# A mixer kernel of two layers: low parts stored a step later, and z updates moved out of the third block product

## The chip, the cores and the metric

The kernel runs on one core of one Trainium2 chip. The metric is the device time of one launch in microseconds, the median of several runs; lower is better. The engines are called as in the profile: PE (matrix products; PEld is its weight load), DVE (vector), ACT (scalar), POOL (GpSimd) and SP (which only issues DMAs here). Each engine works through its own queue in order; a DMA is issued from the queue of SP, POOL or ACT and lands later.

## The reference

```python
def _A_ref(x, wqkv, wo):                       # linear attention, 32 heads of 16
    qkv = (x @ wqkv).reshape(B, S, 3, H, Dh).transpose(2, 0, 3, 1, 4)
    phi = lambda t: jnp.where(t > 0, t + 1, jnp.exp(t)) + 1e-6
    pq, pk = phi(q), phi(k)
    kv = einsum("bhsd,bhse->bhde", pk, v);  z = pk.sum over s
    o = einsum("bhqd,bhde->bhqe", pq, kv) / (einsum("bhqd,bhd->bhq", pq, z) + 1e-6)
    return o.reshape(B, S, D) @ wo

def _B_ref(x, w_in, w_sp, b_sp, w_out):        # gated MLP, mixing over tokens
    z = gelu(x @ w_in)                         # 2048 x 1792
    z1, z2 = z[..., :896], layernorm(z[..., 896:])
    g = einsum("ts,bsf->btf", w_sp, z2) + b_sp # 2048 x 2048 times 2048 x 896
    return (z1 * g) @ w_out

for _ in range(2):                             # two layers, same weights
    x = x + _A_ref(layernorm(x), wqkv, wo)
    x = x + _B_ref(layernorm(x), w_in, w_sp, b_sp, w_out)
```

x is 2048 x 512 in fp32, all weights are fp32.

## The kernel before, in words

Every product is made of three PE matmuls on rounded operands: an operand is split into a high part (ACT, `high`, L223: a copy to fp32r) and a low part (DVE, `low`, L226: the operand minus its high part), and `mm3` (L237 to L239) adds high x high, high x low and low x high in a PSUM bank. Splits that are used more than once can be kept in DRAM and loaded again; those are the arrays `lows` (lowP in the profile).

The order of all instructions is written out by hand: the program is one long list, and each engine takes its share of it in that order. Buffers come from small pools handed out first in, first out: 22 pages (128x512), 6 quads (128x2048), 4 bigs, 8 PSUM banks. The 16 blocks of 128 tokens are called tiles; loops run over steps s, in which different tiles stand at different stages.

Each layer has three phases.

1. Class `P1`, the projection phase: a step per tile with layernorm (`ln_a`, `ln_b`), a turn of the tile through DRAM and DVE's block transposition (`Turn`: the store at L429, the load at L205, `pre` with the transposition at L458), the split of the turned tile (`T_high`, `T_low`), then the products K, Q and Gmm (36 matmuls of 128x512 in a step). In layer two (`self.L` is 1) the loop also makes the low parts of w_sp blocks that the third phase wants: `keepload` (L1671) fetches a quad of w_sp, `keep` makes its high and low part in the next step and stores the low part (L1681), six pieces in all. `wk` and `wq` hold four of the six quads in this loop.
2. Class `P2`, the token steps: attention output, second layernorm, gelu of both halves. `e`/`e2` make z (tiles `ztile[0..15]`, 128x896 each), `e3` its statistics (a square on ACT, L1101, and three small POOL instructions), `e4` normalises it. Layer one runs `run`; layer two runs `run2`, which takes tiles in pairs (`epair` in even steps, `odd` in odd steps; `epair` holds L1036 and L1042, DVE's sums between two groups of PE). Near the end, `first_a`, `first_b`, `T1`, `tail` make the last quarter of the gelu half by a scheme of seven products (Strassen and Winograd). In layer one `FSums` loads pieces of w_in (L205), splits them a step later (L745 to L748) and stores the sums two steps later (L761).
3. Class `P4`, the token mixing w_sp x z2, by seven block products in the order P2, P1, P6, P7, P4, P5, P3. In layer two P2, P1, P4 and P5 are divided again into seven, 14 steps of 12 matmuls each (`mm_div`, `evac_div`); the others have 8 steps of 18 matmuls (`mm`, `evac`). Each step needs a w_sp operand, split or loaded (`wsp`: ACT L1811, DVE L1814, or for kept pieces POOL's DMA L1817), and a z operand (`zsp` for undivided products: ACT L1877, DVE L1879 or L1881). The scheme updates z in place as it goes: in P6 of layer two `zsp` first replaces the second half of z tile k (H2, 384 columns) by H1 - H2 (L1855) and adds H2 of tile k + 8 (L1856), and then splits it. `run` works ahead: `sp(g + 2)` prepares operands two steps on, `zahead` those of the divided products. `tick` multiplies gates in between (POOL L2090 or DVE L2088).

```python
                if not evac_first and not div_first:
                    self.sp(g + 2)
                    self.zahead(g + (3 if p == "P5" or not early and g < 6 else 4))
                self.mm(g)
```

With `div_first` the evacuation of a divided product's last step stands ahead of `sp(g + 2)`; before, that holds in P4 alone.

Of the kernel before, what the change touches and what calls it, by code (L numbers as in the profile page):

```python
# [96 lines left out]
KEPT = ("P7", "P5", "P1")  # L97
KEEP = 1


# [61 lines left out]
def mixer_kernel(ctx: ExitStack, tc: tile.TileContext, x_in, wqkv, wo_d, win1_d, win2_d, wsp_d, bsp_d, wout_d,  # L162
# [300 lines left out]
    class P1:  # L463
# [187 lines left out]
        def run(self, sums):  # L651
            side = deque([self.win2] * NF)
            ND = NT - DEFER
            for s in range(1, NT + 2):
# [46 lines left out]
                if s == 14:  # L701
                    self.wo = quads.get([P, 4, 512])
                    nc.sync.dma_start(self.wo, wo_d.rearrange("(c p) f -> p c f", p=P))
                if s in range(3,NT-1):
                    self.turn.pre(s + 1)
# [3 lines left out]
                if self.L:  # L709
                    sums.keep()  # L710
                    if s >= KEEP:
                        sums.keepload()
                    if s <= NT:
                        sums.halve(40 + (s - 1) // 2, None, (s - 1) % 2)
                    if 9 <= s < NT + 1:
                        sums.halve(28 + (s - 9) // 2, None, (s - 9) % 2)
                    if s <= 4:
                        self.win2.load(2)
                    else:
                        self.win2.piece()  # L720
                    if s == NT - 1:
                        self.win2.sums()
                    if s == NT:
                        self.win2.last()
                    continue
# [113 lines left out]
    class P2:  # L839
# [498 lines left out]
        def run(self, sums):  # L1338
# [4 lines left out]
            for s in range(1, NT + 3):  # L1343
                if s in (15, 16, 17):
                    self.first_a(s - 15)
                self.loadx(s + 1)
                if s < 5:
# [56 lines left out]
                if s >= 3:  # L1404
                    if s < NT:
                        self.e(s - 3)
                        self.e2(s - 3)
                    if s != NT + 1:
                        self.e3(s - 3)
                for _ in range(FONE.get(s, 0)):  # L1410
                    self.f()
                if s in (15, 16, 17):
                    self.first_b(s - 15)
                    self.first_out(s - 15)
                if s - 2 in WADD:
                    self.fsums.store()
                if s in WADD:
                    if not WADD[s]:
                        self.fsums = FSums()
                    self.fsums.load(WADD[s])  # L1420
                if s - 1 in WADD:
                    self.fsums.split(WADD[s - 1])
# [26 lines left out]
        def odd(self, s, p, q, r):  # L1449
# [34 lines left out]
            if s == NT + 1:  # L1484
                self.first_b(1, 2)
                self.T1()

        def run2(self):
# [129 lines left out]
    class Sums:  # L1618
# [3 lines left out]
        def __init__(self):  # L1622
# [9 lines left out]
            for p in DIVIDED[1]:  # L1632
                for q in range(2):
                    for m in range(1, 5):
                        self.halves[p, m, q] = dram.tile([2, P, 512], F32, name=f"h{p}_{m}_{q}")
            self.parts = [(what, p, m, q) for p in ("P4", "P5", "P1") for what in ("copy", "add") for m in (1, 3, 2, 4)
                          for q in range(2)]
            self.unkept, self.split = deque((j, s + 2 * q) for j, s in ((0, 0), (0, 4), (1, 4)) for q in range(2)), None

# [34 lines left out]
        def keep(self):  # L1674

            if self.split is not None:
# [3 lines left out]
                low(r.bitcast(F32R), r, h)  # L1680
                nc.sync.dma_start(at, r)  # L1681
                quads.put(t)
# [60 lines left out]
    class P4:  # L1743
# [81 lines left out]
        def kept(self, g):  # L1825
            p, k = self.steps[g]
            if p not in KEPT or p == "P7" and k < 4 or p == "P1" and not self.L:
                return None
# [10 lines left out]
        def zsp(self, g):  # L1839
# [13 lines left out]
            elif p == "P6":  # L1853
                if "P1" in self.div:
                    nc.vector.tensor_sub(a[:, H2], a[:, H1], a[:, H2])  # L1855
                    nc.vector.tensor_add(a[:, H2], a[:, H2], b[:, H2])  # L1856
                z, sign = a[:, H2], -1.0
# [25 lines left out]
            if tmp is not None:  # L1883
                pages.put(tmp)
            self.z[g] = (h, l)

        def zdiv(self, p, half, side, q, i):
# [497 lines left out]
        def run(self, nxt):  # L2385
# [17 lines left out]
            for g in range(n):  # L2403
                p, k = self.steps[g]
                self.fetch(g + 5)
                evac_first = p == "P6" and k == HT - 1
                div_first = p in self.div and k == 13 and p == "P4"
                if not evac_first and not div_first:
# [12 lines left out]
                if p in self.div:  # L2421
# [7 lines left out]
                    if k == 13 and p == "P4":  # L2429
                        self.gq.extend((n, f) for n in range(2) for f in range(3))  # L2430
                    if p == "P1":
                        if k == 10:
                            self.ask(3)
# [110 lines left out]
```

## Time and profile before

| what | value |
|---|---|
| time, median of 3 runs | 1352.46 us (1351.88 to 1354.0) |
| profiled execution: time, span | 1353.23 us, 1351.4 us |
| granted PE clock | 1.00 of full speed |
| busy share of the span: PE, PEld, DVE, ACT, POOL | 99%, 84%, 79%, 56%, 36% |
| HBM read and written | 224.26 MB, 114.03 MB (250 GB/s) |
| DMA queue of SP and ACT (q1), of POOL (q0): share of 16 DMA engines | 59.6%, 16.1% |
| largest DMA groups of 512 KB | qd<-s x62, qd<-hP x48, qd<-in_wsp_dram x44 |

The profile names an instruction by its line in the listing above (L226), its engine, its operation and its tiles, out<-in: pg are pages, qd quads, bg bigs, z_z a z tile, bank a PSUM bank. A row of a timeline has the start in us from the span's start, the length in us, and in brackets the idle time of the engine before it with the instruction that ended it. A row of waits has the waiting instruction, the one it waited for, the us in total, the number of waits and the longest. Matmuls overlap: each is drawn 0.39 us long though the next starts earlier.

### The profile page before, as it was taken

Reading aid. Unit: us, or ns where it says so; the run is one execution under the profiler, and the core shown is the slowest. Engines: PE = TensorE matmul, PEld = TensorE weight load, DVE = VectorE, ACT = ScalarE, POOL = GpSimd, SP = SyncE. Lnnn points to the kernel's source line nnn. Section 1 sums busy time; section 2 is a strip of 40 time slices with the busy share of each in tenths; the row PEclk is TensorE's granted clock in tenths of the full one; section 3 lists DMA queues with packets and bytes.
Section 4 is the critical chain, followed back from the end, with each engine's and each line's share of the span. In section 5 each row is a group of like instructions: output and inputs, shape, how many; then the busy total and the mean of one; then the engine's idle time right before and its main releaser. Section 6 shows DMA issues by size and latency. Waiting matters only on the chain.

```text
span 1351.4 us, 19331 instructions
## 1 busy us (share of the span) xinstructions
PE 1333.4 (99%) x6493; PEld 1131.2 (84%) x6493; DVE 1073.5 (79%) x1729; ACT 757.0 (56%) x1278; POOL 480.1 (36%) x633
## 2 busy tenths in 40 slices
PE   9999999999999999999998999999999999999999
PEld 7888888888888888889986788888888876888898
DVE  6779866558899689888857778677689879899885
ACT  5764534446742364445666765556688633666454
POOL 3754765533035400302433554554431022112021
PEclk9999999999999999999999999999999999999999
DMA  5898588887889987895988883678768865679354
GB/s 183 287 316 277 189 264 297 285 265 245 256 268 372 316 273 224 286 330 148 203 201 240 205 203 96 215 251 249 242 202 250 258 225 184 176 237 318 129 77 66
DMA packets 183348, 314.43 MB, mean 233 GB/s; under 512 B 15440, under 2 KB 56400, under 8 KB 182864
## 3 DMA queue, kind: packets, MB, share of 16 engines
q1 hardware_dynamic: 161216, 266.65, 59.6%
q0 software_dynamic: 21888, 46.41, 16.1%
q8 instruction: 51, 0.84, 0.3%
q14 instruction: 49, 0.40, 0.1%
q10 hardware_dynamic: 144, 0.13, 0.0%
HBM read 224.26 MB, written 114.03 MB: 250 GB/s over the span
## 4 chain that ended last, share of the span: by engine, by line
PE 84%; DVE 6%; DMA 5%; ACT 2%; issue 1%; SPq 1%; POOL 1%; ACTq 0%; POOLq 0%; DVEq 0%
PE bank L2051 11%; PE bank L2049 11%; PE bank L2050 11%; PE bank L239 10%; PE bank L237 10%; PE bank L238 10%; PE bank L2250 3%; PE bank L2251 3%; PE bank L2252 3%; DMA pg<-xt 2%; DMA yt<-z_y 1%; PE bank L1169 1%; PE bank L1171 1%; PE bank L1170 1%; PE bank L998 1%
## 5 line engine op out<-in xcount | busy, mean ns | idle before, releaser
L2049 PE MATMUL bank<-qd,pg 128*128 128x512 f32 x704 | 274.8, 390 | 4.1 <-ACT pg L1877 1.7
L2051 PE MATMUL bank<-qd,pg 128*128 128x512 f32 x704 | 274.6, 390 | 0.2 <-DVE pg L1879 0.2
L2050 PE MATMUL bank<-qd,pg 128*128 128x512 f32 x704 | 274.0, 389 | 0.0
L1811 ACT ACTIVATE qd<-qd 128x1024 fp32r<-128x1024 f32 x148 | 155.5, 1052 | 87.6 <-PE bank L2051 41.1
L1814 DVE TENSOR_TENSOR qd<-qd,qd 128x1024 fp32r<-128x1024 f32 x132 | 169.5, 1286 | 29.5 <-ACT qd L1811 29.3
L239 PE MATMUL bank<-qd,pg 128*128 128x512 f32 x448 | 174.7, 390 | 0.0
L2049 PEld LDWEIGHTS bank<-qd,pg 128*128 128x128 f32 x704 | 132.1, 188 | 34.0 <-ACT pg L1877 3.7
L2051 PEld LDWEIGHTS bank<-qd,pg 128*128 128x128 f32 x704 | 132.1, 188 | 29.5 <-DVE pg L1881 1.3
L2050 PEld LDWEIGHTS bank<-qd,pg 128*128 128x128 f32 x704 | 132.1, 188 | 27.3
L237 PE MATMUL bank<-qd,pg 128*128 128x512 f32 x264 | 103.5, 392 | 6.5 <-DVE pg L226 6.3
L238 PE MATMUL bank<-qd,pg 128*128 128x512 f32 x264 | 103.0, 390 | 0.0
L239 PEld LDWEIGHTS bank<-qd,pg 128*128 128x128 f32 x448 | 84.1, 188 | 18.0 <-DVE pg L226 0.4
L1712 POOL TENSOR_TENSOR pg<-pg,pg 128x512 f32<-128x512 f32 x48 | 69.7, 1453 | 71.6 <-DVE pg L1879 51.5
L2090 POOL TENSOR_TENSOR bg<-bg,pg 128x512 f32<-128x512 f32 x28 | 49.4, 1767 | 127.0 <-ACT qd L1811 120.7
L372 POOL TENSOR_SCALAR rs<-mv 128x1 f32<-128x1 f32 x76 | 23.6, 311 | 177.3 <-DVE mv L370 173.4
L223 ACT ACTIVATE pg<-pg 128x512 fp32r<-128x512 f32 (+1 forms) x94 | 55.2, 595 | 51.3 <-DVE pg L1908 21.0
L2252 PE MATMUL bank<-wo,qd 128*128 128x256 f32 x288 | 81.4, 283 | 0.0
L2250 PE MATMUL bank<-wo,qd 128*128 128x256 f32 x276 | 78.1, 283 | 0.0
L2251 PE MATMUL bank<-wo,qd 128*128 128x256 f32 x276 | 78.0, 283 | 0.0
L458 DVE STREAM_TRANSPOSE bank<-pg 128x512 f32<-128x512 f32 x58 | 41.5, 716 | 35.6 <-DMA pg<-yt 21.7
L237 PEld LDWEIGHTS bank<-qd,pg 128*128 128x128 f32 x264 | 49.6, 188 | 18.5 <-DVE pg L226 8.1
L226 DVE TENSOR_TENSOR pg<-pg,pg 128x512 fp32r<-128x512 f32 (+1 forms) x92 | 59.7, 658 | 6.2 <-ACT pg L223 5.7
(308 smaller groups left out, 3420.9 us busy)
## 6 DMA issues: line engine op xcount, KB each, us to landing
qd<-s SPq DMA_DIRECT2D x62, 512.0 KB, 4.4
qd<-hP SPq DMA_DIRECT2D x48, 512.0 KB, 4.7
qd<-in_wsp_dram SPq DMA_DIRECT2D x44, 512.0 KB, 4.4
pg<-z SPq DMA_DIRECT2D x56, 256.0 KB, 5.1
pg<-in_wsp_dram SPq DMA_DIRECT2D x52, 256.0 KB, 4.7
s<-pg SPq DMA_DIRECT2D x48, 256.0 KB, 4.4
z<-pg SPq DMA_DIRECT2D x40, 256.0 KB, 3.6
pg<-w POOLq DMA_DIRECT2D x38, 256.0 KB, 5.2
```

The costliest lines, as they stand in the source:

```text
L237: nc.tensor.matmul(out, ah, bh, start=start, stop=False)
L238: nc.tensor.matmul(out, ah, bl, start=False, stop=False)
L239: nc.tensor.matmul(out, al, bh, start=False, stop=stop)
L1712: nc.gpsimd.tensor_tensor(t, a, b, op=OP.add)
L1811: self.mark = nc.scalar.activation(w[:, 0], r, AF.Copy)
L1814: nc.vector.tensor_sub(w[:, 1], r, w[:, 0].bitcast(F32))
L2049: m(out, h[:, o], w[:, 0, j, :], start=start, stop=False, skip_group_check=True)
L2050: m(out, h[:, o], w[:, 1, j, :], start=False, stop=False, skip_group_check=True)
L2051: m(out, l[:, o], w[:, 0, j, :], start=False, stop=stop, skip_group_check=True)
L2250: m(out, A, x, start=start and f == 0, stop=False, skip_group_check=True)
L2251: m(out, A, y, start=False, stop=False, skip_group_check=True)
L2252: m(out, B, x, start=False, stop=stop and f == 2, skip_group_check=True)
```

## The change

Three edits, two of them in layer two alone.

- The projection phase of layer two: `keep` moves ahead of the turn (`turn.pre`) in the step and no longer stores; a new `keepstore`, at that place in the next step, stores the low part and gives the quad back. Five pieces are made instead of six, and `kept` no longer names step 13 of product P1, whose low part is made on DVE when it is used.
- Product P6 of layer two: its two updates of z leave `zsp`. The eight subtractions become `hsub`, two in each of the odd token steps 9, 11, 13 and 15; the eight sums become `hadd`, two in token step 17 and six in steps 1, 2, 4, 5, 7 and 8 of product P1. `div_first` now holds for step 13 of P1 as well.
- The token steps of layer one: the statistics `e3` of tiles 11, 12 and 13 move from the middle of steps 14, 15 and 16 to the start of steps 15, 16 and 17, behind `first_a`; and in steps 13 to 17 the load of w_in pieces stands ahead of the store of the sums.

```diff
+HADD = {1: 2, 2: 3, 4: 4, 5: 5, 7: 6, 8: 7}
...
+                if self.L:
+                    sums.keepstore()
+                    sums.keep()
                 if s in range(3,NT-1):
                     self.turn.pre(s + 1)
...
                 if self.L:
-                    sums.keep()
                     if s >= KEEP:
                         sums.keepload()
...
                 if s in (15, 16, 17):
                     self.first_a(s - 15)
+                    self.e3(s - 4)
...
-                    if s != NT + 1:
+                    if s < 14 or s > NT + 1:
                         self.e3(s - 3)
...
-                if s - 2 in WADD:
-                    self.fsums.store()
                 if s in WADD:
                     if not WADD[s]:
                         self.fsums = FSums()
                     self.fsums.load(WADD[s])
+                if s - 2 in WADD:
+                    self.fsums.store()
...
             if s == NT + 1:
                 self.first_b(1, 2)
                 self.T1()
+                self.p4.hadd(0, 1)
+            elif s >= 9:
+                self.p4.hsub(s - 9, s - 8)
...
-            self.unkept, self.split = deque((j, s + 2 * q) for j, s in ((0, 0), (0, 4), (1, 4)) for q in range(2)), None
+            self.unkept = deque(((0, 0), (0, 2), (0, 4), (0, 6), (1, 4)))
+            self.split, self.due = None, None
...
                 low(r.bitcast(F32R), r, h)
-                nc.sync.dma_start(at, r)
+                self.due = t, at
+
+        def keepstore(self):
+            if self.due is not None:
+                (t, at), self.due = self.due, None
+                nc.sync.dma_start(at, t[:, 0])
                 quads.put(t)
...
-            if p not in KEPT or p == "P7" and k < 4 or p == "P1" and not self.L:
+            if p not in KEPT or p == "P7" and k < 4 or p == "P1" and (not self.L or k == 13):
                 return None
...
             elif p == "P6":
-                if "P1" in self.div:
-                    nc.vector.tensor_sub(a[:, H2], a[:, H1], a[:, H2])
-                    nc.vector.tensor_add(a[:, H2], a[:, H2], b[:, H2])
                 z, sign = a[:, H2], -1.0
...
+        def hsub(self, *ks):
+            for k in ks:
+                a = ztile[k]
+                nc.vector.tensor_sub(a[:, self.H2], a[:, self.H1], a[:, self.H2])
+
+        def hadd(self, *ks):
+            for k in ks:
+                a, b = ztile[k], ztile[k + HT]
+                nc.vector.tensor_add(a[:, self.H2], a[:, self.H2], b[:, self.H2])
...
-                div_first = p in self.div and k == 13 and p == "P4"
+                div_first = p in self.div and k == 13 and p in ("P1", "P4")
...
                     if p == "P1":
+                        if k in HADD:
+                            self.hadd(HADD[k])
```

## The prediction

> **What bounds the kernel now.** I read the page first: busy time by engine, then the chain that ended last, then TensorE's (PE's) waits, then stretches of the timeline around each wait.
>
> ```profile
> span 1351.4 us, 19331 instructions
> PE 1333.4 (99%) x6493; PEld 1131.2 (84%) x6493; DVE 1073.5 (79%) x1729; ACT 757.0 (56%) x1278; POOL 480.1 (36%) x633
> PE 84%; DVE 6%; DMA 5%; ACT 2%; issue 1%; SPq 1%; POOL 1%; ACTq 0%; POOLq 0%; DVEq 0%
> ```
>
> PE is busy for 1333.4 of 1351.4 us, so no edit can win more than some 18 us unless it takes matmuls away, and this one takes none. The chain says where the rest lies: 16% of it runs outside PE, in places where PE just catches up with somebody. What is to be won are PE's waits, all of which the next view names (us in total, times, longest):
>
> ```profile
> PE bank L237 <- DVE pg L226: 6.3, 4, 1.8
> PE bank L2049 <- ACT pg L1877: 1.7, 4, 0.5
> PE bank L2049 <- DVE bg L2109: 1.6, 1, 1.6
> PE bank L239 <- DVE qd L226: 1.0, 1, 1.0
> PE bank L2049 <- DVE bg L1996: 0.8, 1, 0.8
> PE bank L1952 <- DMA qd<-lowP: 0.5, 1, 0.5
> PE bank L2051 <- DVE pg L1879: 0.2, 1, 0.2
> ```
>
> These rows fall into three places. The four waits on the low part of K's operand (L226) are the early steps of layer two's projection phase (class P1). The ones on L1877, L2109, L1996, lowP and L1879 (eight waits, 4.8 us) stand in the block products P1, P6 and P7 of layer two. L239 on L226 (1.0 us) is the last token step but one of layer one's class P2. A wait costs more than its idle time, as PE's own timeline shows:
>
> ```profile
> 707.80 0.39 PE L239 MATMUL bank<-qd,pg 128*128 128x512 f32 x1
> 711.20 0.39 PE L239 MATMUL bank<-pg,pg 128*128 128x512 f32 x1
> 712.91 0.50 PE L237 MATMUL bank<-qd,pg 128*128 128x512 f32 x1 [1.32 <-DVE pg L226]
> 713.25 0.40 PE L238 MATMUL bank<-qd,pg 128*128 128x512 f32 x1
> ```
>
> Fifteen matmuls started from 707.80 to 711.20, one each 0.227 us. The next came 1.71 us later, a loss of 1.48 for 1.32 idle, since the page draws a matmul 0.39 long; and the one after it took 0.34 instead of 0.227. So I add 0.27 us to each wait: 0.16 for overlap and 0.11 for the restart.
>
> **Part A: low parts in the projection phase (keep, keepstore).** In layer two's class P1 each step loads a quad of w_sp, makes its low part (ACT L223, DVE L226) and stores it from SP (L1681). The chain that ended last goes round in it:
>
> ```profile
> 714.47 5.25 DMA pg<-xt
> ...
> 720.37 1.21 DVE qd L226
> ...
> 722.02 0.47 SPq L1671
> ...
> 722.53 0.87 SPq L311
> ...
> 724.04 4.75 DMA pg<-xt
> ```
>
> ```profile
> SPq L1681 <- DVE qd L226: 28.5, 6, 6.8
> DMA to landing us min/median/max: 3.2/3.5/4.5
> ```
>
> The turned block lands, DVE turns it (L458), the low part stands behind that on DVE, the store waits for it at the head of SP's queue (28.5 us for six stores), and the load of the next turned block stands behind the store. One round takes 9.6 us (714.47 to 724.04), while a step is 36 matmuls, 8.2 us on PE. This is the whole of the four waits. The change breaks it in two places. The low part is made ahead of the turn, so it no longer waits for the block, and T's low part is no longer 1.2 us behind it. The store goes out a step later, when its low part is long done, so SP does not wait for DVE there.
>
> What is late next: the quads. Four of six hold wk and wq, two go round. Before, a quad was stored a step ahead of its next load; now store and load of one buffer follow each other on SP, and the load (L1671) has to wait until the store has landed, 3.5 us by the row above (the second line there is of the stores L1681). That holds in steps 3, 4 and 5. Behind it stand the two w_in loads, x's load and the load of the turned block. The new round goes over two steps. Landing of the block 5.0, from its turn to the store of the block two on 5.4 (L458 at 709.63, L429 at 715.00), then on SP 0.37 for that store, as much for the keep's, the landing L, 0.47 for L1671, and 1.5 from there to the block's next load (722.53 to 724.04):
>
> ```profile
> 709.63 0.73 DVE L458 STREAM_TRANSPOSE bank<-pg 128x512 f32<-128x512 f32 x1 [3.45 <-DMA pg<-xt]
> 715.00 0.37 SPq L429 DMA_DIRECT2D xt<-pg  x1
> ```
>
> That is 13.1 + L; with L at 3.5 a round of 16.6 for two steps, 8.3 each, 0.1 over PE's 8.2, over three held steps some 0.4 us, and with L at 4.5 1.9 us. The sixth piece falls away, with a load and a store of 512 KB, a high part and a low part of 1.2 us; its cover was DVE's step at 747, where the fourth wait stood. The four waits cost 6.3 + 4 x 0.27 = 7.4; I leave 1.5 in place, nearer to the upper case, since the store now runs among the same step's loads, and take **-5.9** (ends: -7.4, and -4.4 if L goes a little over 4.5).
>
> **Part B: z updates and P1's last evacuation, layer two.** In P6 the subtraction and the sum stood in front of each step's high part:
>
> ```profile
> 1108.59 1.23 DVE L1814 TENSOR_TENSOR qd<-qd,qd 128x1024 fp32r<-128x1024 f32 x1 [0.39 <-ACT qd L1811]
> 1109.73 1.65 DVE L1855 TENSOR_TENSOR z_z<-z_z 128x384 f32<-128x384 f32 x1
> 1111.41 0.56 DVE L1856 TENSOR_TENSOR z_z<-z_z,z_z 128x384 f32<-128x384 f32 x1
> 1112.00 0.52 ACT L1877 ACTIVATE pg<-z_z 128x384 fp32r<-128x384 f32 x1 [3.45 <-DVE z_z L1856]
> 1112.43 1.04 ACT L1811 ACTIVATE qd<-qd 128x1024 fp32r<-128x1024 f32 x1
> 1113.64 2.31 DVE L1814 TENSOR_TENSOR qd<-qd,qd 128x1024 fp32r<-128x1024 f32 x1
> ```
>
> A round of low part, subtraction, sum, z's high part, w's high part and again the low part: 5.05 us from 1108.59 to 1113.64, against 18 matmuls, 4.1 us on PE. With L1855 and L1856 gone the high parts on ACT wait for nothing of DVE, and the round falls apart into 1.6 us on ACT and, on DVE, L1814 at 1.2 to 2.3 and the remaining 0.56 (L1881), at most 2.9, or 3.6 in the steps that add a bias of the size of one L1996 (0.7). So P6 should run at PE's pace, and DVE should be free when P6 ends (L2109). L1996 is product P1's last evacuation, which waited behind a step of P6's z work; now it comes ahead of it and PE, which needs that bank only nine matmuls later (2.0 us), should not wait. Eight waits: 4.8 + 8 x 0.27 = 7.0. I leave 0.6 for the start of P7, whose z work is unchanged, and take **-6.4** (ends -7.0 and -3).
>
> The price of the dropped piece comes due in step 13 of product P1: POOL's load of 512 KB, for which PE waited 0.5, gives way to one low part on DVE, 1.2 us as L1814 above, made two steps ahead of its use in a stretch where DVE stood idle 3.80 us:
>
> ```profile
> 1087.98 1.37 DVE L1996 TENSOR_TENSOR bg<-bg,bank 128x512 f32<-128x512 f32 x2 [3.80 <-PE bank L2051]
> ```
>
> So it costs nothing; without that cover it would cost its 1.2 us.
>
> Where the updates go: six sums of 0.56 into steps 1 to 8 of product P1, two subtractions (1.1 us) into each of the token steps 9, 11, 13 and 15, two sums into step 17.
>
> ```profile
> 1059.00:1081.00 22.00, 22.00 (x99) 18.22 (x98) 18.50 (x33) 13.87 (x23) 1.63 (x3) 1.00 0.76 240
> 887.02 0.63 DVE L1036 TENSOR_TENSOR bank<-bank,z_z 128x448 f32<-128x448 f32 x1 [2.58 <-ACT bank L1035]
> 990.28 0.62 DVE L1036 TENSOR_TENSOR bank<-bank,z_z 128x448 f32<-128x448 f32 x1
> 991.49 1.23 DVE L226 TENSOR_TENSOR qd<-qd,qd 128x1024 fp32r<-128x1024 f32 x1 [0.58 <-ACT qd L223]
> 991.80 0.36 PE L998 MATMUL bank<-bg,bg 128*128 128x448 f32 x1
> 993.31 0.47 PE L998 MATMUL bank<-bg,qd 128*128 128x448 f32 x1
> ```
>
> In product P1 (first row: stretch, length, then busy us of PE, weight load, DVE, ACT, POOL) DVE is busy 18.5 of 22 us; 3.3 more just fit, and DVE works two steps ahead there: nothing (uncovered, 3.3). After the token steps 9 to 13 DVE idles 2.58 us ahead of L1036: nothing (uncovered, 1.1 each). Step 17 has no cover. The two sums start where L1036 did, at 990.3, so L1036 ends at 992.0 instead of 990.9, and PE's group at 991.80 needs it; then L226 ends at 993.3 and L1042, as long as L1036, at 993.9, and PE's group at 993.31 comes at about 994.0. That is 0.7, and the 1.1 of step 15 reaches the same chain in part. I take **+1.0** (ends: +0.5, and +2 if both arrive whole).
>
> **Part C: layer one's P2.** The squares e3 of tiles 11 to 13 move behind first_a of the next step, and the win loads go ahead of the stores on SP:
>
> ```profile
> 306.56 2.08 SPq L761 DMA_DIRECT2D w1s<-pg  x4
> 308.68 1.99 SPq L205 DMA_DIRECT2D pg<-in_win_dram  x2
> 314.40 0.42 DVE L745 TENSOR_TENSOR pg<-pg 128x256 f32<-128x256 f32 x1 [2.79 <-DMA pg<-in_win_dram]
> 319.73 0.68 DVE L226 TENSOR_TENSOR qd<-bank,qd 128x512 fp32r<-128x512 f32 x1
> ```
>
> DVE waited 2.79 us for those loads and then worked without a pause up to the low part at 319.73 for which PE waited. Loads 2.1 us earlier pull this by about 2 us; the wait costs 1.0 + 0.27 = 1.3, and I take **-1.3** (ends -1.3 and 0). The squares keep their length and move into idle time of ACT; the stores go out some 1 to 2 us later, and their reloads come steps after.
>
> **The sum.** -5.9 - 6.4 + 1.0 - 1.3 = -12.6 us. The profiled execution took 1353.23 us for a span of 1351.4 and would take 1340.6. It stands 0.8 above the median of 1352.46, so against that 1339.9; I say 1340.
>
> **The rivals.** *The store's landing takes the place of the low part.* If transfers in these steps take longer than their median, the new round stays near the old 9.6. Part A then gives 2.5 instead of 5.9: 1343 to 1344. For it: the hold at L1671 is certain and three steps long; against it: the row's longest landing is 4.5. The Trainium skill (DMA: Bandwidth & Descriptors, Anatomy of one DMA — SWDGE (gpsimd) path) has it that DMA engines do not wait on semaphores and the issuing sequencer does; by that rule the hold stands in SP's queue and costs what this rival says, and the trace agrees with 28.5 us of such waits.
>
> *P6 stays bound by DVE.* L1855 took 1.65 where L1856, of the same size, took 0.56, and L1814 took 2.31 at 1113.64 instead of 1.23, both while POOL ran a gate. If each P6 step pays both that and a second such stretch, DVE needs 3.6 + 1.1 = 4.7 against 4.1, eight steps keep some 4.5 of 7.0, and the time is about 1344. Against it: one gate runs per step. The Trainium skill (SBUF — State Buffer, Who interferes with whom) says that a VectorE instruction with two SBUF inputs contends with a GpSimd one that reads SBUF, the later waiting for the whole of the first; by that rule the wait goes over from the removed subtraction to the low part that stays, and the trace agrees (1.65 and 2.31). That alone keeps DVE at 3.6.
>
> *The change does not do what it says:* PE, ahead by 13 us, catches up with another engine right behind, and the time is given back, about 1350 to 1352. Against it: no other row of PE's waits stands between these places.
>
> *Slower.* The hold on SP decides alone if landing L is long: three held steps lose 1.5 x (L - 3.2), by the round above. To eat the 6.7 of the other parts and 2.7 more on top of the 7.4 lost today, it must lose some 17 us, L near 14.5, four times the median: 1355 or more.
>
> **How the numbers follow.** My forecast, with its own range of 1336.5 (all ends at their best, -15.2 us, give 1337.3) to 1343, has a chance of 0.63; the two rivals near 1344 have 0.15 and 0.11, and both together reach 1347; given back 0.06; slower 0.03; 0.02 lies below 1336.5. The range 1336.5 to 1347.5 takes in the first three. About 0.2% (2.7 us) is what a measurement of this kernel can tell from no change: faster 0.93 (the first three, what lies below, and a third of the case given back), same 0.04, slower 0.03.
>
> **What would show it.** PE's waits on L226 in class P1 fall below 2 us, SP waits at L1671 instead of L1681; L1877's row is gone from PE's waits and P6 runs at 4.1 us a step; a new wait of about 0.7 us on L1036 or L1042 stands near 990; layer one's wait of 1.0 us on L226 is gone. The prediction is wrong if PE waits in class P1 stay above 4 us, or if new ones appear in the token steps or in product P1.

## The result, and the profile after

The changed kernel took 1341.03 us (median of 5 runs, 1338.87 to 1342.81) beside 1352.46 for the kernel before, a ratio of 0.9913 [0.9898, 0.9927]: 11.4 us faster, against 1340.0 predicted (1336.5 to 1347.5). Five more runs on another occasion gave 1338.49 (1337.59 to 1342.66) beside 1354.46, ratio 0.9891 [0.9874, 0.9907]. (The ratios are those on record; they go by all runs of both sets and are not the quotients of the medians, which are 0.9915 and 0.9882 here.) The profiled execution below took 1342.81 us, the slowest of the first five, for a span of 1341.0, against 1353.23 and 1351.4 before.

First the page's head and busy time, and the engine shares of the chain that ended last:

```profile
span 1341.0 us, 19334 instructions
PE 1330.3 (99%) x6493; PEld 1131.2 (84%) x6493; DVE 1076.6 (80%) x1729; ACT 756.0 (56%) x1277; POOL 483.8 (36%) x632
PE 83%; DMA 6%; DVE 4%; ACT 2%; SPq 2%; issue 1%; POOL 1%; POOLq 0%; DVEq 0%; ACTq 0%
```

The number of matmuls is the same and no engine does notably less; the shares of the chain hardly move either. Neither view shows where 10 us went. PE's waits do (us in total, times, longest):

```profile
PE bank L238 <- DVE pg L227: 3.2, 3, 2.1
PE bank L2072 <- ACT pg L1888: 0.9, 1, 0.9
PE bank L394 <- DVE pg L384: 0.9, 1, 0.9
PE bank L2074 <- DVE pg L1890: 0.4, 1, 0.4
PE bank L2072 <- DVE bg L2019: 0.4, 1, 0.4
PE bank L1001 <- DVE z_z L1045: 0.2, 1, 0.2
```

(Lines have moved: L227 is the low part, L226 before; L1888 and L1890 are z's high and low part, L1877 and L1879 before; L1045 is L1042 before.) In layer two's class P1 two of the four waits are left, 2.12 and 0.66 us (the third of that row, 0.4, stands near the program's start, at 23.2). Of the eight in the products none is left in P1 or P6, but a new one, 0.94 with 0.45 behind it, stands at the start of P7, at its second step (the expectations below call it the first). The wait of layer one's step 16 is gone. Token step 17 shows a new one of 0.2. L394 (start of the program) and the 0.4 on L2019 (layer one's products) stand in code that the change does not touch.

Behind the two waits in class P1 stand SP's waits in that stretch, and the landing times of its deferred stores (the row of L1695):

```profile
SPq L430 <- ACT pg L382: 16.8, 7, 4.8
SPq L1679 <- DMA lowP<-qd: 16.6, 3, 7.2
```

```profile
L1695 SPq DMA_DIRECT2D lowP<-qd x5: 458/478/827, 703.9 to 740.9; - x5
...
DMA to landing us min/median/max: 3.6/5.7/7.7
```

SP no longer waits at the store for DVE (28.5 us before); it waits three times at the load of the quad (L1679) until the store of the same buffer has landed. That is the hold that the prediction named, but a landing now takes 3.6 to 7.7 us where it took 3.2 to 4.5. SP's timeline shows it step by step:

```profile
711.84 0.53 SPq L1695 DMA_DIRECT2D lowP<-qd  x1
719.59 0.37 SPq L1679 DMA_DIRECT2D qd<-in_wsp_dram  x1
721.52 0.39 SPq L430 DMA_DIRECT2D xt<-pg  x1
722.01 0.48 SPq L1695 DMA_DIRECT2D lowP<-qd  x1
729.14 0.37 SPq L1679 DMA_DIRECT2D qd<-in_wsp_dram  x1
```

Store 711.84, next load 719.59, 7.7 us later; store 722.01, load 729.14, 7.1 later. PE's two waits end at 729.17 and 738.28, 9.6 and 9.1 us behind these loads. The trace points to the place in the queue. Before, the store of 711.49 went out with none of SP's transfers under way and the step's loads behind it, from 711.91 on, and it landed after 3.4 us. Here six transfers go out ahead of the store of 711.84, from 707.58 to 711.42; they land in their order from 713.15 to 717.00, and the store last, at 719.57. The chain that ended last shows how the second wait follows: the landing of the store of 722.01, the quad's load at 729.14, its high part, its low part at 733.99, the turn at 735.21, and PE at 738.28. As the low part now stands ahead of the turn, a quad that comes late holds the turn back too.

P6 runs at PE's pace. The row gives the stretch, its length, and the busy us of PE, weight load, DVE, ACT and POOL:

```profile
1098.00:1122.00 24.00, 24.00 (x107) 19.90 (x106) 18.45 (x21) 6.13 (x9) 8.08 (x4) 1.00 0.62 208
```

107 matmuls in 24 us, none waiting, and DVE at 18.45 of 24. Then comes P7:

```profile
1119.96 0.60 ACT L2130 ACTIVATE bg<-bank 128x512 f32<-128x512 f32 x1 [5.70 <-PE bank L2074]
1122.00 0.60 ACT L2130 ACTIVATE bg<-bank 128x512 f32<-128x512 f32 x1 [1.44 <-PE bank L2074]
1122.49 1.05 ACT L1825 ACTIVATE qd<-qd 128x1024 fp32r<-128x1024 f32 x1
1123.58 1.23 DVE L1828 TENSOR_TENSOR qd<-qd,qd 128x1024 fp32r<-128x1024 f32 x1 [1.57 <-ACT qd L1825]
1123.62 2.33 POOL L2113 TENSOR_TENSOR bg<-bg,pg 128x512 f32<-128x512 f32 x1 [10.40 <-ACT qd L1825]
1124.72 1.65 DVE L1875 TENSOR_TENSOR pg<-z_z 128x384 f32<-128x384 f32 x1
1126.40 0.52 ACT L1888 ACTIVATE pg<-pg 128x384 fp32r<-128x384 f32 x1 [2.86 <-DVE pg L1875]
1126.98 0.50 PE L2072 MATMUL bank<-qd,pg 128*128 128x512 f32 x1 [0.94 <-ACT pg L1888]
```

The kernel makes the operands for P7's second step only after P6's last evacuation (on ACT L2130, at 1119.96 and 1122.00), by a condition named evac_first. Before the change no wait stood there, since PE had just waited 1.6 us for that evacuation. Now PE reaches P7 earlier and needs z's high part while ACT, which had idled 5.70 us, has only just begun the round. The subtraction in it takes 1.65 instead of 0.55 us beside POOL's gate, as in P6 before; these 1.1 us are more than the wait of 0.94, so another place for the gate might have done as well, which no run tests.

### The profile page after: what moved, and what is told of

The parts are those of the page before. It is cut to its first block, busy times and chain, and to the rows that moved or that the text cites. A ratio compares the mean times of both kernels' runs of the same rounds, so it can differ in the third digit from the quotient of the medians.

```text
span 1341.0 us, 19334 instructions
## 1 busy us (share of the span) xinstructions
PE 1330.3 (99%) x6493; PEld 1131.2 (84%) x6493; DVE 1076.6 (80%) x1729; ACT 756.0 (56%) x1277; POOL 483.8 (36%) x632
## 4 chain that ended last, share of the span: by engine, by line
PE 83%; DMA 6%; DVE 4%; ACT 2%; SPq 2%; issue 1%; POOL 1%; POOLq 0%; DVEq 0%; ACTq 0%
PE bank L2074 12%; PE bank L2072 12%; PE bank L2073 11%; PE bank L240 9%; PE bank L238 9%; PE bank L239 9%; PE bank L2273 3%; PE bank L2274 3%; PE bank L2275 3%; DMA yt<-z_y 2%; PE bank L1174 1%; PE bank L1172 1%; PE bank L1173 1%; PE bank L1001 1%; PE bank L1002 1%
## 5 line engine op out<-in xcount | busy, mean ns | idle before, releaser
L2074 PEld LDWEIGHTS bank<-qd,pg 128*128 128x128 f32 x708 | 132.9, 188 | 28.5 <-DVE pg L1890 0.9
L2113 POOL TENSOR_TENSOR bg<-bg,pg 128x512 f32<-128x512 f32 x28 | 53.2, 1903 | 122.8 <-ACT qd L1825 121.0
L227 DVE TENSOR_TENSOR pg<-pg,pg 128x512 fp32r<-128x512 f32 (+1 forms) x92 | 59.9, 659 | 6.5 <-ACT pg L224 5.6
L238 PEld LDWEIGHTS bank<-qd,pg 128*128 128x128 f32 x264 | 49.6, 188 | 14.9 <-DVE pg L227 4.5
```

Of the source, the lines that this page charges most:

```text
L238: nc.tensor.matmul(out, ah, bh, start=start, stop=False)
L2074: m(out, l[:, o], w[:, 0, j, :], start=False, stop=stop, skip_group_check=True)
```

## The experiments

The time of one execution of such a kernel varies by several us, so each trace was also laid beside that of the kernel before matmul for matmul (all have 6493): how much earlier the n-th starts, at both ends of a stretch. The difference of the two is what PE gained there (us, minus is a gain; the stretches are class P1 of layer two, 710 to 757 by the clock of before; from the end of the token steps to P7's second step, 997 to 1141, where all of it arises from P1's last step on; layer one's steps 235 to 323; token step 17, 982 to 997). Each row is one execution, and so is the base: its wait near 320 is 1.04 us, with part A or part B alone, which don't touch that code, 0.53 and 0.66.

| execution | class P1 | P6 and its ends | 235 to 323 | step 17 |
|---|---|---|---|---|
| changed kernel, first trace | -4.2 | -5.9 | -0.5 | +0.3 |
| changed kernel, second trace | -6.6 | -5.9 | -1.8 | +0.3 |
| part A alone | -5.3 | 0.0 | +0.5 | 0.0 |
| part B alone | +1.0 | -5.9 | -0.1 | +0.4 |
| part C alone | +3.2 | 0.0 | -1.8 | 0.0 |
| part C's loads alone | +2.1 | 0.0 | -1.3 | 0.0 |
| changed, low part stored at once | -5.5 | -5.9 | -1.8 | +1.0 |
| changed, low part behind the turn | -4.8 | -5.9 | -1.8 | +0.3 |
| changed, both of these | -1.8 | -5.9 | -1.9 | +0.4 |
| changed, store issued earlier | -5.9 | -5.9 | -1.8 | +0.9 |
| changed, P7's operands ahead | -5.4 | -7.9 | -1.8 | +0.3 |
| changed, last evacuation behind | -5.9 | -5.9 | -1.9 | +0.6 |
| changed, stored at once and P7's operands ahead | -5.8 | -7.9 | -1.8 | +0.3 |

**The parts alone.** Each is the kernel before with one part of the diff, hunks as in the diff above.

Part A: keepstore and keep ahead of the turn, pieces, kept().

> The kernel before with part A alone (low part made ahead of the turn, stored a step later; sixth piece dropped); parts B and C as before. The prediction said -5.9 us. The trace of the whole change reads about -4.1 for the same stretch, because two of the four waits on the low part in class P1 of layer two are left (2.12 and 0.66 us). Theory 1 (the held load of the quad keeps them): -4 to -4.5 us, ratio 0.9967 to 0.9970, with waits of 2.5 to 3.2 us left in class P1, and the held loads landing-bound in SP's waits. Theory 2 (the parts share their gain: PE runs ahead of another engine only when all parts are in): less than -3 us here. Theory 3 (the prediction's own size was right and the whole change loses something elsewhere): -5.5 or more, and less than 2 us of waits left.

Measured 1347.31 us, ratio 0.9957 [0.9943, 0.997]: 5.8 us faster by the ratio, 5.0 by the medians (1352.33 before, beside it). PE's waits (the page of this kernel) keep one on L226 in class P1, and the products' waits stay (L2057 is L2049 before, L2004 is L1996):

```profile
PE bank L2057 <- ACT pg L1885: 1.6, 4, 0.5
PE bank L2057 <- DVE bg L2117: 1.6, 1, 1.6
PE bank L2057 <- DVE bg L2004: 1.6, 1, 1.6
PE bank L237 <- DVE pg L226: 1.6, 1, 1.6
```

PE gains 5.3 us in class P1. The waits left, 1.6 us, are theory 3's, the prediction's own size; theory 1, built on the one trace of the changed kernel, asked for 2.5 to 3.2 us and was too pessimistic. The time alone, uncertain by 1.8 us either way, can't tell -4.5 from -5.5. Idle time fell by 4.7 with three waits fewer: with 0.27 each that is 5.5.

Part B: hsub, hadd, P6 without the two updates, div_first for product P1.

> The kernel before with part B alone (z updates of layer two out of P6 into the token steps and product P1; product P1's last evacuation ahead of the next step's operands). The prediction said -6.4 and +1.0 for token step 17, so -5.4 together. The trace of the whole change reads -5.9 and +0.2. Theory 1: -5.5 to -6 us, ratio 0.9956 to 0.9959; P6 without a wait on z's high part; waits of 0.9 and 0.4 us left at the first step of P7; in token step 17 a wait of 0.1 to 0.8. Here class P1's waits stay as before (6.3 us), so PE comes to step 17 about 4 us later against the other engines and the wait there should, if anything, be smaller. Rival (the updates cost DVE time where they go): waits of over 1 us in the token steps or in product P1, and -4.5 or less.

Measured 1348.15 us, ratio 0.9963 [0.9949, 0.9977]: 5.0 us faster by the ratio, 4.2 by the medians. The trace has theory 1's waits, 0.94 and 0.45 at P7, 0.17 in step 17, and none in P1, P6 or the other token steps. PE gains 5.9 us around P6 and loses 0.4 in step 17. The rival found nothing.

Part C: e3 and window loads in layer one's P2; then its loads alone.

> The kernel before with part C alone (layer one's class P2: the squares of tiles 11 to 13 behind first_a of the next step, window loads ahead of the stores). The prediction said -1.3. Theory 1 (trace of the whole change: the wait of 1.0 near 320 goes, but about 0.7 comes back near 312): -0.5 us, ratio 0.9996, which the time alone can hardly tell from nothing; in the trace PE's wait on the low part near 320 is gone, and a loss of 0.5 to 0.8 us stands near 311 to 315. Rival (the loss near 312 belongs to the run, not to the change): no loss there, -1.3 us, ratio 0.9990.

> The kernel before with one half of part C alone: the window loads ahead of the stores on SP, the squares where they were. Read in the trace, since the time can't tell 1 us. Theory 1 (the loads are the whole of part C, as the prediction has it): the loads go out about 2 us earlier, VectorE's wait for them near 312 is below 1 us instead of 2.79, and TensorE's wait on the low part near 320 (1.04 before, 0.53 and 0.66 in the two kernels without part C beside it) is gone. Rival (the squares in front of the high part on ScalarE hold it): the loads are early and VectorE does not wait for them, but TensorE's wait near 320 stays at 0.5 us or more, now behind the high part on ScalarE.

```
-                if s - 2 in WADD:
-                    self.fsums.store()
                 if s in WADD:
                     ...
                     self.fsums.load(WADD[s])
+                if s - 2 in WADD:
+                    self.fsums.store()
```

Part C alone measured 1351.39 us, ratio 0.9997 [0.9987, 1.0007]: nothing that the time can tell; the loads alone were run once, at 1353.15. In both traces the wait near 320 is gone, and PE gains 1.8 us by 323 with part C and 1.3 with the loads alone. It does not lose 0.7 near 312; there the rival of the first text is right. With the loads alone they go out at 306.12 instead of 308.68, and the first instruction that waited 2.79 us for them starts at 311.38 without a wait:

```profile
306.12 0.90 SPq L205 DMA_DIRECT2D pg<-in_win_dram  x2
311.38 0.42 DVE L745 TENSOR_TENSOR pg<-pg 128x256 f32<-128x256 f32 x1
317.94 0.69 DVE L226 TENSOR_TENSOR qd<-bank,qd 128x512 fp32r<-128x512 f32 x1
```

The low part starts 1.8 us earlier (319.73 before; PE has 0.45 of that as a lead already at 235), and PE does not wait for it: the loads are enough, as theory 1 has it. Whether the squares are the 0.5 between the two traces stays open. But at the end of both executions the lead is mostly lost. It goes at one place, behind the fourth wait of class P1, which part C leaves in. PE's timeline of the loads-alone kernel there, and its stretches (the eighth column is the granted TensorE clock):

```profile
747.57 0.39 PE L239 MATMUL bank<-pg,pg 128*128 128x512 f32 x1
749.96 0.50 PE L237 MATMUL bank<-qd,pg 128*128 128x512 f32 x1 [2.00 <-DVE pg L226]
...
751.72 0.63 PE L237 MATMUL bank<-qd,pg 128*128 128x512 f32 x1
752.14 0.63 PE L238 MATMUL bank<-qd,pg 128*128 128x512 f32 x1
```

```profile
751.40:754.20 2.80, 2.80 (x8) 2.21 (x7) 0.94 (x2) 2.29 (x4) 2.10 (x2) 0.50 0.50 141
754.60:757.00 2.40, 2.40 (x12) 1.93 (x11) 2.37 (x5) 1.86 (x4) 0.00 (x0) 1.00 1.04 233
```

After an idle time of 2.00 us (3.22 in the trace of part C) matmuls start 0.43 us apart instead of 0.227, for 3.4 us, and PE loses 1.5 more. So the +2.1 and +3.2 of these two rows in class P1 are no cost of part C, and its worth is read where it acts.

**What in part A does the work.** The changed kernel once more, with its two halves undone one at a time and then together, and one that issues the deferred store earlier.

> The changed kernel itself once more, as a base for the three variants beside it. Its traces so far: two waits on the low part left in class P1 (2.1 and 0.7 us), deferred stores landing after 3.6 to 7.7 us, waits of 0.9 and 0.4 us at the first step of P7 in layer two. Theory 1 (how many of class P1's waits are left depends on how long each deferred store takes to land, and that differs from one execution to the next): ratio 0.9913 again within its interval, and in the trace waits of 1 to 3 us in class P1, with the longest behind the store that lands last. Rival (the two waits belong to the order of the instructions): the same two steps, 2.1 and 0.7 us within 0.2.

Measured 1338.49, ratio 0.9891 [0.9874, 0.9907]. In class P1 one wait of 0.2 us is left, below theory 1's 1 to 3, and the landings were shorter:

```profile
PE bank L238 <- DVE pg L227: 0.2, 1, 0.2
```

```profile
DMA to landing us min/median/max: 3.6/4.9/5.5
```

The same program, another execution: the waits are not in the order of the instructions (the rival falls) but come and go with the landings. Over the traces with deferred stores in their old place, the longest landing and PE's waits in class P1 (us) rise together but for the last two: 5.5 and 0.2; 6.6 and 1.0 (last evacuation behind); 7.3 and 1.4 (P7's operands ahead); 7.4 and 1.6 (part A alone); 7.7 and 2.8; 8.1 and 2.1 (low part behind the turn).

> The changed kernel with the deferred store of the low part issued some instructions earlier in the step, ahead of the store of x's block for which SP waits on ACT (16.8 us over seven such waits in class P1). Theory 1 (the held load of the quad waits for the landing of that store, 3.6 to 7.8 us, and this is what keeps two of the four waits in class P1): the landing now runs beside SP's wait for ACT, the waits on the low part in class P1 fall from 2.8 to below 1 us, and the time falls by 2 to 3 us more, ratio to the kernel before about 0.989 to 0.990 against 0.9913 for the changed kernel. Rival (the landing is long because the store shares the DMA engines with the same step's loads): it lands no earlier, the waits stay between 2 and 3 us, ratio 0.9913. Second rival (the round through x's block and its turn sets the pace, not the quad): the landing goes out of SP's waits, but the waits of PE stay.

```
+                if self.L:
+                    sums.keepstore()
                 if s <= NT:
                     self.K_phi(s - 1)
...
-                    sums.keepstore()
                     sums.keep()
```

Measured 1338.39, ratio 0.989 [0.9875, 0.9905], with 1.1 us of waits left and landings no shorter:

```profile
DMA to landing us min/median/max: 4.1/6.0/9.5
```

The time is where theory 1 put it, yet the changed kernel itself reached the same in its second set, so this tells nothing from no change. The waits fell nearly as theory 1 said, and SP's waits for the landing from 16.6 to 13.4 us, but the store itself lands no sooner: it still goes out behind loads.

> The changed kernel with the low part made ahead of the turn, as there, but stored at once in the same step, so that SP waits at the store for DVE as before the change, and the held load has a step for the landing. Theory 1 (the deferral is needed: the store behind a low part that waits for its quad's landing holds the loads behind it on SP): waits on the low part in class P1 of 3 to 6 us against 1 to 3 with the deferral, ratio about 0.993 to 0.995. Rival (making the low part ahead of the turn is all that counts, and the deferral only makes the landing late): waits below 1.5 us, ratio 0.989 to 0.990, stores landing after 3.2 to 4.5 us as before the change.

```
-                self.due = t, at
+                nc.sync.dma_start(at, t[:, 0])
+                quads.put(t)
```

Measured 1339.66, ratio 0.989 [0.9877, 0.9904], against 0.9891 for the changed kernel beside it. Two waits, 1.1 us together, and the short landings are back:

```profile
DMA to landing us min/median/max: 4.2/4.3/4.8
```

The rival is right: with the low part ahead of the turn the deferral isn't needed.

> The changed kernel with the low part made behind the turn again, as in the kernel before, but its store deferred to the next step. Theory 1 (both halves of part A count about alike: T's low part, which TensorE waits for, does not stand on DVE 1.2 us behind the quad's): in class P1 the quad's low part is again ahead of T's on DVE, each of four steps is up to 1.2 us later, and the waits are 4 to 6 us against 1 to 3, ratio 0.9935 to 0.995. Rival (the round through SP's queue was the whole limit, and DVE's order does not matter once the store is deferred): waits of 1 to 3 us as in the changed kernel, ratio 0.9913.

```
-                    sums.keep()
                 if s in range(3,NT-1):
                     self.turn.pre(s + 1)
...
                 if self.L:
+                    sums.keep()
```

Measured 1340.4, ratio 0.9897 [0.9884, 0.9911], 2.1 us of waits. Again the rival: with the store deferred, the low part may stand behind the turn.

> The changed kernel with both halves of part A undone (low part behind the turn again, stored at once again), so that of part A only the dropped sixth piece is left. Each half alone has kept class P1's waits on the low part at 1.1 us (stored at once) and 2.1 us (made behind the turn). Theory 1 (either half alone breaks the round through SP's queue, and with both undone the round is back): three waits of 1.3 to 1.7 us in class P1 return, the fourth, behind the sixth piece, stays away; 4.5 us of waits, about 5 us slower than the changed kernel beside it (median 1338.5 to 1341 so far), so 1343 to 1346, ratio 0.993 to 0.995. Rival (the sixth piece, with its load and store of 512 KB and its 2.4 us on ACT and DVE, was what kept the round long): waits of 1 to 2.5 us, ratio 0.989 to 0.991.

(Both of the last two edits.) Measured 1343.69, ratio 0.9932 [0.9918, 0.9946], as theory 1 had it. PE's waits in class P1, and SP's there:

```profile
PE bank L238 <- DVE pg L227: 4.5, 3, 1.9
```

```profile
SPq L1690 <- DVE qd L227: 24.1, 5, 6.6
```

Three waits and SP's long waits for DVE are back, the fourth stays away. The dropped piece alone gives PE 1.8 us in class P1; one half added to it makes 5.5 or 4.8, and both 4.2 to 6.6: the second half adds nothing that these runs can show.

**What in part B does the work.**

> The changed kernel with one condition changed in layer two: the operands for the second step of P7 are made ahead of P6's last evacuation again, instead of behind it. Theory 1 (the 1.3 us that part B gives back at P7's first step comes from that order alone: z's high and low part wait for the evacuation on ACT and DVE, while both idle 3 to 6 us just ahead of it): the waits of 0.94 and 0.45 us at P7's first step go, -1.4 to -1.9 us, ratio 0.0010 to 0.0014 below the changed kernel beside it. Rival (the evacuation is what PE needs next, and goes late behind the operands): the two waits go and one of about 1.5 us on the evacuation takes their place; no gain, or a loss of up to 1 us.

```
-                evac_first = p == "P6" and k == HT - 1
+                evac_first = p == "P6" and k == HT - 1 and not self.L
```

Measured 1338.49, ratio 0.9886 [0.9869, 0.9903], beside 0.9891 [0.9874, 0.9907]: the time can't tell the two apart. The trace can. PE has no wait at P7 and gains 7.9 us around P6 where the kernels with part B and P7's old order gain 5.9; z's high part now comes ahead of both parts of the evacuation on ACT:

```profile
1115.77 0.53 ACT L1888 ACTIVATE pg<-pg 128x384 fp32r<-128x384 f32 x1 [2.90 <-DVE pg L1875]
1117.62 0.60 ACT L2130 ACTIVATE bg<-bank 128x512 f32<-128x512 f32 x1 [1.32 <-PE bank L2074]
1119.66 0.60 ACT L2130 ACTIVATE bg<-bank 128x512 f32<-128x512 f32 x1 [1.44 <-PE bank L2074]
```

Theory 1's mechanism is shown, its effect on the time is not: class P1 waited 1.4 us in this trace and 0.2 in that one.

> The changed kernel with product P1's last evacuation behind the next step's operands again, the z updates staying where the change put them. Theory 1 (this wait was on the evacuation's place in DVE's order, not on the z updates): a wait of TensorE on that evacuation returns at P6's start, but shorter than the 0.8 to 1.6 us of the kernels with the updates in P6, since DVE no longer has the two updates (2.2 us) in front of it: 0.3 to 0.8 us, too little for the time to show (ratio within 0.001 of the changed kernel's 0.989 to 0.991). Rival A (without the updates the order does not matter): no wait. Rival B (it matters in full): 1.6 us and a ratio 0.0012 higher.

```
-                div_first = p in self.div and k == 13 and p in ("P1", "P4")
+                div_first = p in self.div and k == 13 and p == "P4"
```

Measured 1340.64, ratio 0.9909 [0.9893, 0.9924], and no wait at all on L2019 at P6's start. Rival A: DVE, without the updates, comes to the evacuation in time; it even idles before it.

```profile
1087.07 1.37 DVE L2019 TENSOR_TENSOR bg<-bg,bank 128x512 f32<-128x512 f32 x2 [0.86 <-PE bank L2074]
```

**A version put together from these.**

> The version that the runs point to: the changed kernel with the low part stored at once (which did without the deferral, with waits of 1.1 us in class P1) and with the operands of P7's second step made ahead of P6's last evacuation (which took 1.9 us off the end by the trace). Theory 1 (the two add up): no wait at P7's first step, 0 to 1.1 us left in class P1, 1336.5 to 1338.5 against 1338.5 to 1341 for the changed kernel, ratio 0.988. Rival (a saving at P7 is given back further on, or the waits of class P1 are drawn anew in each execution and decide): the changed kernel's time within 1 us, ratio 0.989 to 0.991.

Measured 1338.62 (1336.85 to 1339.17), ratio 0.9893 [0.9879, 0.9908]. The trace is as theory 1 says, no wait at P7 and 0.8 us in class P1, with the shortest span of all, 1335.0 us. By the time it is the rival that stands: it beats the kernel before, but is not told from the changed kernel.

## Why the prediction came out right, step by step

**The sum.** -12.6 us was predicted against the profiled execution; the span fell by 10.4 in the first trace and 14.9 in the second, -10.3 and -14.0 of it in the table's four places. The parts alone, -5.8, -5.0 and -0.4 by the ratios, add up to -11.2 (by the medians to -10.1), against -11.8 (-11.4) for the whole: no dependence of one on another is to be seen, though each figure is uncertain by 1 to 2 us. That the sum came so near is in part luck: part B was taken 0.5 too large and step 17 0.7 too dear, which cancel, and part A differs by 2.4 us between two executions of one kernel.

**Part A, -5.9.** Alone -5.8 by the ratio, -5.0 by the medians and -5.3 by the trace; in the two traces of the changed kernel -4.2 and -6.6. The size was right. Two of its steps were not. "In two places" puts one price on two breaks of the round; the runs show that either is enough, and that 1.8 of the gain is the dropped piece's, so the round was not "the whole of the four waits" (the fourth goes with the piece alone). And the landing was mis-sized: L was taken as 3.5, at most 4.5, from stores that went out ahead of their step's loads. Stored at once they still land in 4.2 to 4.8; deferred, they go out behind loads and land in 3.6 to 8.1. The prediction saw this ("the store now runs among the same step's loads") and left 1.5 us for it; 0.2 to 2.8 came. By its formula, three held steps losing 1.5 x (L - 3.2), the first trace's median of 5.7 gives 3.8, against 2.8 idle and 2 x 0.27, 3.3; the second's 4.9 gives 2.6, and 0.2 was seen, so as a price it is an upper one. The rival named for the landing came half true in the first trace, whose waits of 2.8 us stand between the forecast's "below 2" and "above 4". Its rule (the Trainium skill, DMA: Bandwidth & Descriptors, Anatomy of one DMA — SWDGE (gpsimd) path) bears up: the hold stands in SP's queue, as 16.6 us at L1679.

**Part B, -6.4.** It is -5.9 in every kernel that has it with P7's old order. All eight waits went: PE gained 7.2 us up to P7's second step, against 7.0 in the prediction, and gave 1.3 back there, against 0.6. The term that was mis-sized is "0.6 for the start of P7, whose z work is unchanged": the work is unchanged, but PE comes earlier, the waits there are 0.94 and 0.45, and taking them away was worth 2.0. The reason given for L1996's wait was that the evacuation comes ahead of P6's z work. It was not needed: with the old order and the updates gone there is no wait. The wait of 0.5 on lowP has no price of its own: with part C alone, which still loads that piece, it is gone too, and the next wait, on L1996, is 1.6 instead of 0.8. The low part made in its place cost nothing, as forecast: part A alone shows 0.0 in this stretch.

The updates cost nothing in product P1 either. These are the changed kernel's rows for the work of the stretch that the prediction showed, which now stands 4.7 us earlier, and for the fullest one, just behind it:

```profile
1054.26:1076.26 22.00, 22.00 (x99) 18.23 (x98) 20.03 (x37) 13.55 (x22) 1.64 (x3) 1.00 0.73 239
1059.00:1081.00 22.00, 22.00 (x98) 18.21 (x97) 22.00 (x40) 14.11 (x21) 2.10 (x3) 1.00 0.77 252
```

DVE is busy 20.03 of 22 us instead of 18.50, then 22.00 of 22, and PE has no gap in either: "just fit", in the second with nothing to spare.

**Step 17, +1.0.** It costs 0.3 in both traces of the changed kernel (0.3 to 1.0 in the others that have it). The chain is the one that was named, sums, L1039 (L1036 before), low part, L1045:

```profile
985.26 1.02 DVE L1908 TENSOR_TENSOR z_z<-z_z,z_z 128x384 f32<-128x384 f32 x2
987.87 0.62 DVE L1045 TENSOR_TENSOR z_z<-bank,z_z 128x448 f32<-128x448 f32 x1
988.40 1.22 DVE L1179 TENSOR_TENSOR qd<-qd,qd 128x1024 f32<-128x1024 f32 x1
```

L1045 ends at 988.49 and PE goes on at 988.54; with the 5.02 us that it was ahead at 982 it would have gone on at 988.29. Most of the 0.3 arises one group earlier, behind L1039. The sums came whole, but from their start to L1045's it took 2.61 us, while the lengths that the prediction adds come to 2.97: DVE's rows overlap by about 0.1 us each. That is the step that was mis-sized; and the share added for step 15 did not come.

**Part C, -1.3.** It is worth 1.8 in every trace that has it whole but the first of the changed kernel, where only 0.5 came of it: 0.7 of the gain of 1.2 was lost again near 312, where a low part came late. Part A without C loses 0.5 in this stretch, so that is no cost of part C. It gave more than "the wait plus 0.27", which the prediction took as its best end, because it also took away a wait of 0.2 us at 317, which cost 0.4 to 0.5 with its restart. That row (L1169 on ACT's L1186) is one of four that the prediction's list of PE's waits leaves out, though it calls the list complete. By the time of part C alone none of it is shown.

**The rival of a P6 still bound by DVE** fell: 18.45 of 24 us. What it was drawn from was real and moved on to P7's subtraction (1.65 beside the gate). **Given back** came true on a small scale at P7: 1.3 us, and taking the two waits away was worth 2.0. **Slower** had no support.

## What to carry to other kernels

Where a wait goes round through several engines, one cut is often enough; try each alone before keeping both, since the second can bring costs of its own, here a store that lands later because it goes out behind loads. A duration read from transfers that go out first is a lower end once they are moved behind others. And when a bound engine gets faster, look at the next order that was chosen for its old lateness: P6's evacuation first brought no wait at P7's second step as long as PE came late (the other order was not run in the kernel before).

## What the runs showed of the hardware

An idle time of PE can cost more than itself. After 2.00 and 3.22 us of idleness the granted clock stood at 0.50 for 3.4 us and 1.5 us more were lost; after 2.12 (the changed kernel, 729.17) and 2.50 us (part B alone, 752.23) it stayed at 1.00. Length alone does not decide. The Trainium skill (TensorE: Matmul & The Clock Gate, Part 1: The HAM clock gate) has the clock set by a free-running activity window of about 3.4 us, in which an idle window halves it. The halving and its length agree; but no idle time here filled such a window, so the idle share that is enough must be smaller. The traces show where the windows fall: in all fourteen, every later change of the granted clock lies a whole number of 3.413 us after its first rise to 1.00. On that grid the 2.00 us lie within one window (747.71 to 751.13) and are 0.59 of it, and the 3.22 us are 0.94 of one; the clock drops at that window's end. The 2.12 and the 2.50 us are each divided between two windows, at most 0.48 of one. The largest idle share of a window after which the clock stayed at 1.00 is 0.52 (1.76 us, the changed kernel with both halves of part A undone). Two drops are few, but all idle times of these traces, by the lengths as drawn, fit a limit between 0.52 and 0.59 of a window.

Ten runs of the changed kernel spread over 5.2 us. Its two traces differ by 4.5 us of span: 0.8 in the program's first 25 us, 1.3 between 235 and 323, 0.6 more by 470 and 2.5 in class P1, of which the second trace loses 1.1 again behind it. Differences of 1 or 2 us between two such kernels have to be read at the place where they arise.
